# Another order of the first pieces of a linear-attention and mixture-of-experts kernel

## The chip, the cores and the metric

One core of a Trainium2 chip runs one program. The metric is the device time of the whole program in microseconds. The engines named below are TensorE (PE, its weight loads PEld), VectorE (DVE), ScalarE (ACT), GpSimd (POOL) and SyncE (SP), which here issues every DMA.

## The reference

A gated linear attention (4 batches, 8 heads, 768 tokens, head size 48) gives 3072 rows of 384 numbers. They go through a mixture of 8 experts whose mixing weights come from a gate, normalised by turns over rows and columns (8 times):

```python
for t in range(S):
    state = alpha[:, :, t, :, None] * state + np.einsum('bhd,bhe->bhde', k[:, :, t], v[:, :, t])
    y[:, :, t] = np.einsum('bhd,bhde->bhe', q[:, :, t], state)
x = y.transpose(0, 2, 1, 3).reshape(B * S, H * D)      # 3072 x 384
logits = x @ w_gate
P = np.exp(logits - logits.max())
for _ in range(8):
    P /= P.sum(1, keepdims=True) + 1e-09
    P /= P.sum(0, keepdims=True) + 1e-09
    P *= N / E
for e in range(8):
    out += P[:, e:e+1] * (np.maximum(x @ w1[e], 0.0) @ w2[e])   # w1 384x1024, w2 1024x384
```

## The kernel before, in words

**Attention.** The tokens are cut into units of 256 (3 for each of 4 batches) and these into chunks of 128 tokens, 24 in all. Chunks 0 to 3 (the first two units) are made by `direct_chunk`, step by step: the loads of alpha, k, q and v (`AN`, `KN`, `QN`, `VN`); the *turn*, in which TensorE transposes alpha, k and q into `psD`, `psTk`, `psQR`, ScalarE copies them out, and VectorE forms T = q times decay; six *levels* of 1 to 32 tokens, each with matmuls into `psl`, two products of T with the decay D, a predicated copy of the level's scores into A, and a *merge* that multiplies neighbouring decays (D2 from D1, and so on); level 64 with ScalarE's copies of A; the tail (`psy`, ScalarE's `ab` and `kb`); the normalisation and the carried state `ST`; the transposed x (`xT`); and the gate's matmul `psg`. The later chunks take their scores from *block units*: `attn_block` (b2, b3, ...) loads q, alpha and k of a unit as `qt`, `al`, `kt`, forms 16 products of neighbouring tokens (`tmp`, on GpSimd), which VectorE sums into `AB`, and multiplies decays into qt and kt.

**Experts.** The weights of the first three experts are loaded in the attention's time by `load_expert`: w1 and w2 through buffers named `xT`, squares on ScalarE, a scale s_w, and then four pieces of w1 and four of w2, each split into an upper half in float16 and the *lower half*, what the upper half lost. The lower half is made by VectorE (scalar_tensor_tensor), or by ScalarE and GpSimd. `work_gate` does the same with the gate's weights: a load `wgf`, its largest entry `wgm`, a scale, and the halves `wg`. `moe_tile` multiplies x by w1 and, after the ReLU, by w2, for 128 or 256 tokens at a time (`ps` matmuls); these tiles are what TensorE works on when nothing of the attention is ready.

**The order.** The program is written out by one string, `ORDER` (line 40). Its entries are called one after the other: `c0` the next step of chunk 0, `b2` of block unit 2, `w0` of expert 0's weights, `g` of the gate, `d3` the decays of unit 3, and `f` gives 0.45 us worth of tiles, if tiles are there. An entry in upper case sets `lop[0]`, which moves what may be done by either engine from VectorE to GpSimd: lower halves, merges of D, products of blocks. An entry that may not come yet (`early_`) is kept and tried again before each later one. Every engine runs its own instructions in the order in which they were written, and waits where an operand or a buffer isn't ready.

Of the kernel before, what the change touches and what calls it, by code (L numbers as in the profile page):

```python
# [25 lines left out]
def tile_gla_moe(ctx: ExitStack, tc: tile.TileContext, q, k, v, alpha, wg, w1, w2, out):  # L26
# [10 lines left out]
    NTT = NT // P  # L37
    NP = H // 2
    DP = 64
    ORDER = 'W1 C0 c1 C0 c0 f f f w1 f f f W0 f g f f f f f f f f w0 f f c0 f w0 c0 C1 C0 c1 C0 w0 c0 f f c1 f c2 C0 f f b2 b2 f f f f f f f w2 W0 f c1 w2 c1 f f f w0 b2 f f f C2 f f f f f f f f f f f f f f f f f f B2 f f f f f f f f f f w0 w0 w0 f f C3 f W2 c0 f f c1 c1 f f f f f f c1 C2 B2 b3 b2 f f C1 c2 d2 C0 C2 w2 f f f f f f C1 C0 C1 B2 f f f f c2 B2 f g f b2 f f w0 f f f f f f f f f f f f f f f f f f f f f f f f f f f f f f f f f f f f f f f f f f f f f f f f f f f f f f f f f f f f f f f f W0 f f f f f f f f f f f f f f f f f f f f f f f f f f f f f f f f f f f f f f f f f f f f f f f f f f f f f f f f f f f f f f f f f f f f c3 f f f f f f f f f f f f f f f f f f f f f f f f f f f f f f f f f f f f f f f f f f f f f f f f f f f f f f f f f f c2 f f f f f f C0 w2 w2 w2 W2 C3 f f f f f f f w0 f f f f f f f f f f f f f f f f f f f c2 f f f f f f f f f f f f f f f f f f f f f f f f f f f f f f f f f f f f f f f f f f f f f f f f f f f f f f f f f f f f f f f f f f f f C3 f f f f f f f f f f f f f f f f f f f f w1 f f f f f f f f f f f f f f f f f f f f f f f f f f f f f f f f f f C3 f f f f f f f f f f f f f f f f f f f f f f f f f f f f f f f f f f f f f f f f f f f f f f f f f f f f f f w0 f f f f f f f f f f f f f f f f f f f f f f f c2 f f f f f f f f f f f f f f f f f f f f f f f f f f f f f f f f f f f f f f f f f f f f W0 f B3 B3 C2 f f f C2 f f f f w0 b2 C2 f f f f f f g f f f C3 f W1 f f f f f f f f f f f f f f f f f f f f f f f f f f f f f b2 C1 f f f f f f f f f f f f f f f f f f f f b2 f f W0 f f f f f f f f f f f f f C3 f f f c3 f f b3 B2 f B2 W0 f f f B2 C4 C3 f f f f f f w1 f f g w2 D3 f f c3 c3 C3 w1 C2 f f f w1 f w1 f f f f f f f f f f f f f f B2 f W1 f f f b3 W1 f f f f f f f w1 f f f f f f f f c4 f f W1 f f w1 f f f B3 B3 W1 f f f f f f f f f f f f f f f f f f f f f f f f f f f f f f f f f f f f f f f f f f f f f f f f f f f f f f f f f f f f f f f f f f f f f f f f f f f f f f f f f f f f f f f f f f f f f f f f f f f f f f f f f f f f f w1 f f f f f f b4 f f f f f f f f c4 f f f f f f f f f f f f f f f f f f f f c4 f f f f f f f f f f f f f f f f f f f f f f f f f f f f f f f f f f f f f f f f f f f f f f f f f f f f f f f f f f f f f f f f f f f f f f f f w1 f f f f f c3 f f f f f f f f f f b3 f f c4 f f f f f f f f f f f f f f f f B3 f f f f f f f f B3 f c6 c5 B3 f f f b3 w2 f f f f f f b3 f f f f f b3 c4 f B3 f f w2 f c5 w2 f f f w2 f f f w2 c5 w1 C5 w2 f f f f f f f f f f f f f f f f f f c5 f f f f f f w2 f f f f f f B3 B4 f f f f f f f f f f f f f f f f f b4 f b4 f f f f f f f f f f f f f f b4 f f f f b4 b4 f f B4 f B4 c5 f f f f f f f f f f f b4 f B4 c6 f b4 f f f C8 f f f c6 f f B4 f f B4 C6 f f f f f c6 B4 f c7 B5 B4 f f f f c6 f c7 f f f f f f d4 f f f f f f f c7 f f c7 f f f f f f f f f b5 f C7 B5 b5 f f c8 f f f f C7 B5 f f f f f f f f f f b5 b5 f f f f f f f f f f f f f C9 f f c8 f f f f f f f B5 f f f f f f f b5 f f f f B5 B5 f f f t f b5 f f b5 f f f f f b5 f f b5 f f f f c8 c8 B5 c9 f f f f f f t c9 f f f B6 f f f f c9 f f f f f d5 f c8 f f f c9 f f f c10 f f f f f c9 f f f f c10 b6 f f f f f f f f b6 f f t f f f B6 f b6 f B6 f t f f f f f f f f B6 f f f f f f f c11 f f c10 f f f f f f f B6 f f f f f f f f f t f f b6 f f B6 f f f f b6 B6 f f f B6 b6 f b6 b6 B7 f f f f c10 f c11 f f f f f f f f t f f c11 f f f f c10 f f c11 f f f f f d6 f f f f c11 c12 f f f f f f f f c11 f f f f C12 c10 f f f b7 f f f f f f B7 f t f f B7 B7 f f f f f t f f B7 f f f f f f b7 f f f f f f f f c13 f f f c12 B7 f f f f f f f f f f B7 f f f f f f f f b7 f B7 f f f f B7 f f f B7 b7 f f b7 f f f c12 f c13 f f f f f f b7 f B8 c13 f f f f f f f c12 f f c13 f f f f d7 f f f f f c13 f f f f f c14 f f C13 f f f f C14 c12 f f f f f f f f b8 f f f f f f b8 f b8 B8 f f f f f B8 f f f f f f b8 f f c15 f f c14 f f f f f f B8 f f f f f f b8 f f f t f f f f B8 f f f f b8 f b8 f f B8 f B8 b8 f f f f f f B9 b8 f f c14 f c15 f f f f f f t c15 f f f f f f c14 f c15 f C15 f f f f f d8 f f f f B9 c16 f f f f f f f f c15 f f f f c16 c14 f f f f f b9 f f f f f f t f B9 f f B9 f f f B9 t f B9 f f f f f f f f f f f f f c17 f f c16 f f f f f f B9 f f f f f b9 f f f t f f f f B9 f f C17 f b9 B9 f f f b9 f f B9 b9 f f f b9 f f f f c16 f f f t f f f f B10 c17 f c16 f f f f f c17 f f f f f f d9 f f c17 f c18 f f f B10 f f f f f f c17 f f f f c16 c18 f f f f f f f b10 f f f f f t f f f B10 f f B10 f b10 t f f f f f f f b10 f f f f f f f f c19 f f f f f f f f f B10 f f f f f b10 f f f t f f f c18 f B10 B10 f f f f f b10 f B10 f f f B10 f f f f f f c18 b10 f c19 B10 f f f f t B11 c19 f f f f f f c18 f f c19 f f f f f f d10 f f f f c19 c20 f f f f f f f f c19 f f f f c20 c18 f f f f f f f f b11 f f f f f B11 f b11 f B11 f B11 b11 f f f f f f f f f f f f f f c21 f f c20 f f f f f f f B11 f f f f f b11 f f f t f f f f B11 f f f f b11 B11 f f b11 f f B11 b11 f f b11 f f f f f c20 f c21 f f f f f f t v c21 f f f f f f c20 f f c21 f f f f f d11 f f f f c21 c22 f f f f f f f f c21 f f f f c22 c20 f f f f f f f f f f f f f f f f f f f f f f f f f f f f f f c23 f f c22 f f f f f f f f f f f v f f f f t f v f f f f f f f f v f v f f f f f v f v f f f c22 f c23 f f f f f v f t v c23 f f f f f f c22 v f f c23 f f f f v f f f v f f c23 f f f f f v f f f c23 f f f f c22 f f f f f f f f f f f f f f f f'  # L40
    NA = 3

    pin = tc.keep_in_program_order
# [847 lines left out]
    w0, w1_, w2_ = (load_expert(e, wAB[e]) for e in range(NA))  # L891
# [85 lines left out]

    order = ORDER.split()
    while order:
# [582 lines left out]
```

## Time and profile before

| | us |
|---|---|
| median of three runs | 1655.36 |
| lowest and highest | 1650.81, 1655.67 |
| profiled execution | 1653.3 |
| its span in the trace | 1651.6 |
| TensorE busy in the span | 1596.8 (97%) |
| VectorE busy | 1271.7 (77%) |
| ScalarE busy | 930.8 (56%) |
| GpSimd busy | 375.1 (23%) |

The span is the time from the first to the last instruction that the profiler recorded; the execution's own time is 1.7 us longer. TensorE is busy in nearly all of it; the page's 40 slices show it less busy in the first three only (6, 6 and 8 tenths, at granted clocks of 6, 6 and 8 tenths), which is where attention and weights have to be made before tiles exist.

### The profile page before, as it was taken

How to read it: one execution, taken by the hardware profiler on the slowest of the kernel's cores; microseconds unless marked ns; L12 is line 12 of the kernel's file. 1: busy time of each engine (PE TensorE's matmuls, PEld its weight loads, DVE VectorE, ACT ScalarE, POOL GpSimd, SP SyncE). 2: the span in 40 equal slices, each digit the busy share in tenths (PEclk: the TensorE clock that was granted, in tenths of full speed). 3: DMA queues.
4: the chain of work that ended last, by engine and by line, in shares of the span. 5: the costliest groups of instructions: out<-in, count | busy, mean ns of one | idle time of the engine just before them, and what ended most of it. 6: DMA issues, size and time to landing. Idle time of an engine off the chain costs nothing.

```text
span 1651.6 us, 45345 instructions
## 1 busy us (share of the span) xinstructions
PE 1596.8 (97%) x18865; PEld 1376.3 (83%) x18865; DVE 1271.7 (77%) x2854; ACT 930.8 (56%) x2230; POOL 375.1 (23%) x382
## 2 busy tenths in 40 slices
PE   6689999999999999999999999999999999999999
PEld 5567777777777777777799999999999999999998
DVE  6868667665666666447778988998799879999997
ACT  4257543433443343434677777766776677665554
POOL 2325366557457656310000000000000000000000
PEclk6689999999999999999999999999999999999999
DMA  7244431542353343322253263235323543325443
GB/s 169 54 114 116 104 80 53 133 122 67 76 122 84 105 116 75 89 73 107 55 184 103 103 177 121 94 129 170 129 94 129 154 138 100 119 96 183 151 151 126
DMA packets 194655, 188.53 MB, mean 114 GB/s; under 512 B 115088, under 2 KB 175248, under 8 KB 194448
## 3 DMA queue, kind: packets, MB, share of 16 engines
q1 hardware_dynamic: 194448, 185.62, 38.1%
q8 instruction: 148, 2.42, 0.6%
q14 instruction: 59, 0.48, 0.1%
HBM read 129.76 MB, written 55.82 MB: 112 GB/s over the span
## 4 chain that ended last, share of the span: by engine, by line
PE 80%; DVE 10%; POOL 2%; ACT 2%; SPq 2%; issue 2%; DMA 1%; DVEq 0%; ACTq 0%; POOLq 0%
PE ps L66 28%; PE p1a L66 15%; PE p2x L66 12%; PE p2y L66 6%; PE p1c L66 4%; PE p1d L66 4%; PE p2v L66 3%; PE psy L66 2%; SPq L57 2%; PE psl L66 2%; DVE h L57 2%; POOL tmp L57 2%; DVE w L57 1%; DVE AB L57 1%; DVE hf L57 1%
## 5 line engine op out<-in xcount | busy, mean ns | idle before, releaser
L66 PEld LDWEIGHTS <-h 128*128 128x128 f16 x6768 | 593.1, 98 | 117.4 <-issue 6.7
L66 PEld LDWEIGHTS <-w 128*128 128x128 f16 x4896 | 464.2, 98 | 64.5 <-issue 13.4
L57 DVE TENSOR_TENSOR h<-hf,h 128x256 f16<-128x256 f32 x480 | 286.4, 616 | 31.8 <-ACT h L57 31.4
L66 PE MATMUL ps<-xT,w 128*128 128x256 f16 (+1 forms) x2664 | 300.0, 270 | 5.1 <-DVE h L57 3.6
L66 PE MATMUL ps<-w,h 128*128 128x384 f16 x1728 | 296.7, 327 | 2.3 <-POOL w L57 1.2
L66 PE MATMUL p1a<-x,w 128*128 128x256 f16 (+1 forms) x1860 | 289.3, 269 | 5.1 <-DVE p1d L57 3.0
L66 PE MATMUL p2x<-w,h 128*128 128x192 f16 x2832 | 272.0, 246 | 0.0
L57 ACT CAST h<-hf 128x256 f16<-128x256 f32 x480 | 250.7, 571 | 14.3 <-DVE hf L57 10.2
L57 DVE TENSOR_TENSOR hf<-hf 128x256 f32<-128x256 f32 x480 | 182.1, 420 | 29.7 <-ACT hf L57 24.9
L66 PE MATMUL p1a<-x,wx 128*128 128x256 f16 (+1 forms) x744 | 199.6, 269 | 0.0
L57 DVE SCALAR_TENSOR_TENSOR h<-ps,h 128x256 f16<-128x256 f32 (+1 forms) x296 | 114.5, 410 | 101.9 <-ACT h L57 100.9
L57 ACT ACTIVATE h<-ps 128x256 f16<-128x256 f32 (+1 forms) x296 | 110.4, 377 | 140.2 <-PE ps L66 139.4
L66 PEld LDWEIGHTS <-wx 128*128 128x128 f16 x1736 | 167.3, 98 | 17.3
L57 POOL TENSOR_TENSOR tmp<-qt,kt 128x768 f32<-128x768 f32 (+2 forms) x83 | 137.8, 1665 | 134.8 <-DMA kt<-in_k_dram 50.3
L57 ACT ACTIVATE hf<-p1d 128x256 f32<-128x256 f32 x120 | 46.0, 383 | 164.2 <-DVE h L57 140.5
L66 PE MATMUL p2y<-w,h 128*128 128x192 f16 x1416 | 136.1, 246 | 0.0
L57 DVE TENSOR_REDUCE AB<-tmp 128x16 f32<-128x768 f32 (+2 forms) x90 | 81.1, 903 | 68.6 <-POOL tmp L57 68.4
L57 ACT COPY r<-ps 128x384 f32<-128x384 f32 x72 | 34.3, 478 | 163.7 <-PE ps L66 129.5
L66 PE MATMUL p1c<-x,wx 128*128 128x256 f16 (+1 forms) x372 | 98.8, 269 | 0.0
L66 PE MATMUL p1d<-x,wx 128*128 128x256 f16 (+1 forms) x620 | 85.2, 269 | 0.0
L57 ACT ACTIVATE hf<-p1c 128x512 f32<-128x512 f32 x120 | 70.9, 591 | 0.0
L57 ACT COPY A<-psl 16x128 f32<-16x128 f32 (+3 forms) x148 | 49.2, 335 | 35.1 <-PE psl L66 30.7
(229 smaller groups left out, 1946.4 us busy)
## 6 DMA issues: line engine op xcount, KB each, us to landing
x<-xd SPq DMA_DIRECT2D x60, 704.0 KB, 5.4
accd<-acc SPq DMA_DIRECT2D x48, 384.0 KB, 3.2
acc<-accd SPq DMA_DIRECT2D x48, 384.0 KB, 3.2
raw<-r SPq DMA_DIRECT2D x72, 192.0 KB, 1.9
ri<-raw SPq DMA_DIRECT2D x72, 192.0 KB, 3.9
xT<-in_moe_w_dram SPq DMA_DIRECT2D x8, 768.0 KB, 5.0
w1f<-in_moe_w_dram SPq DMA_DIRECT2D x16, 384.0 KB, 7.5
w2f<-in_moe_w_dram SPq DMA_DIRECT2D x8, 768.0 KB, 6.9
```

The lines of the kernel that those rows point to most:

```text
L57: r = f(*a, **k_)
L66: tc.keep_in_program_order(nc.tensor.matmul(out_, lhsT, rhs, start=start, stop=stop, **k_))
```

## The change

Only the string changes. Its first entries (1150 before, 1900 now; the difference is 750 more `f`, which do nothing while no tile waits) are in another order; each chunk, block, expert and the gate has as many entries as before, and the last 1225 entries are the same. Some are in upper case that were not, and the other way round.

```diff
-    ORDER = 'W1 C0 c1 C0 c0 f f f w1 f f f W0 f g f f f f f f f f w0 f f c0 f w0 c0 C1 C0 c1 C0 w0 c0 f f c1 f c2 C0 f f b2 b2 f f f f f f f w2 W0 f c1 w2
...
+    ORDER = 'w2 W2 C0 f f C0 f f f f f w2 f f f D2 f f f f f f c4 f B2 f f f f f f f f f f f f f f f f f f f f f f f f w2 f f f f f f f f f f f f f f f f 
...
```

The order of SyncE's transfers at the start. AN, KN, QN, VN are a chunk's alpha, k, q, v; the buffers xT0_1, xT1_1 take an expert's w1, xT0_2, xT1_2 its w2; qt, al, kt are block unit 2's. Before:

```order
L57 DMA xT1_1_86<-in_moe_w1_dram 32x1024 x4
L57 DMA wgf_197<-in_moe_w_gate_dram 32x3x8 x4
L57 DMA xT0_2_84<-in_moe_w2_dram 128x4x384
L57 DMA xT1_2_87<-in_moe_w2_dram 128x4x384
L57 DMA AN_155<-in_alpha_dram 128x8x48
L57 DMA KN1_120<-in_k_dram 128x8x48
L57 DMA QN1_118<-in_q_dram 128x8x48
L57 DMA VN1_125<-in_v_dram 128x4x48 x2
L57 DMA qt_0_2_522<-in_q_dram 128x1x768
L57 DMA al_0_2_524<-in_alpha_dram 128x1x768
L57 DMA kt_0_2_523<-in_k_dram 128x1x768
```

After, from the same queue:

```order
L57 DMA VN0_124<-in_v_dram 128x4x48 x2
L57 DMA qt_0_2_230<-in_q_dram 128x1x768
L57 DMA al_0_2_232<-in_alpha_dram 128x1x768
L57 DMA kt_0_2_231<-in_k_dram 128x1x768
L57 DMA wgf_197<-in_moe_w_gate_dram 32x3x8 x4
L57 DMA AN_155<-in_alpha_dram 128x8x48
L57 DMA KN0_119<-in_k_dram 128x8x48
L57 DMA QN0_117<-in_q_dram 128x8x48
L57 DMA VN0_124<-in_v_dram 128x4x48 x2
```

Block 2's three loads moved from behind chunk 2's to directly behind chunk 0's; w1 moved behind the gate and chunk 1, w2 further back.

VectorE, at expert 0's second pair of w2 pieces (w21 is the lower half, T and A32 are levels of chunk 2 and 3, AB the sums of block 2). Before, from the last rows of chunk 3's level 4:

```order
L57 COPY_PREDICATED A32_0_3_1119<-odd_165,psl1_0_3_1102 128x64x2
L57 TENSOR_TENSOR T1_0_3_1061<-T1_0_3_1061,D4_0_3_1173 128x2x32x4
L57 SCALAR_TENSOR_TENSOR w21_0_297<-xT0_2_84,s_w2_0_1150,w20_0_296 128x768
L57 TENSOR_TENSOR T0_0_2_652<-T0_0_2_652,D64_0_2_1152 128x2x2x64
L57 COPY_PREDICATED A32_0_2_751<-odd_165,psl_0_2_734 128x8x32
L57 TENSOR_TENSOR T1_0_2_653<-T1_0_2_653,D64_0_2_1152 128x2x2x64
L57 TENSOR_TENSOR D128_0_2_1219<-D64_0_2_1152 128x4
L57 SCALAR_TENSOR_TENSOR w21_0_297<-xT1_2_87,s_w2_0_1150,w20_0_296 128x768
L57 TENSOR_REDUCE AB0_126<-tmp8_0_2_6_1022 128x4x8
L57 TENSOR_REDUCE oneg_wg_1283<-pst_wg_1280 1x1
L57 TENSOR_SCALAR oneg_wg_1283<-oneg_wg_1283 1x1
L57 TENSOR_SCALAR one_wg_1282<-oneg_wg_1283 1x1
```

After:

```order
L57 TENSOR_TENSOR T0_0_2_705<-T0_0_2_705,D64_0_2_1209 128x2x2x64
L57 COPY_PREDICATED A32_0_2_742<-odd_165,psl_0_2_725 128x8x32
L57 TENSOR_TENSOR T1_0_2_706<-T1_0_2_706,D64_0_2_1209 128x2x2x64
L57 TENSOR_TENSOR T0_0_3_965<-T0_0_3_965,D8_0_3_1164 128x2x16x8
L57 COPY_PREDICATED A32_0_3_1075<-odd_165,psl0_0_3_1057 128x32x4
L57 COPY_PREDICATED A32_0_3_1075<-odd_165,psl1_0_3_1058 128x32x4
L57 TENSOR_TENSOR T1_0_3_966<-T1_0_3_966,D8_0_3_1164 128x2x16x8
L57 TENSOR_REDUCE AB0_126<-tmp4_0_2_5_1187 128x4x4
L57 TENSOR_TENSOR qt_0_2_230<-qt_0_2_230,al_0_2_232 128x2x192
L57 TENSOR_TENSOR al_0_2_232<-al_0_2_232 128x2x48
L57 TENSOR_TENSOR tmp8_0_2_6_1283<-qt_0_2_230,kt_0_2_231 128x1536
L57 SCALAR_TENSOR_TENSOR w21_0_385<-xT0_2_84,s_w2_0_1238,w20_0_384 128x768
```

The gate's four steps on `oneg_wg` and `one_wg` are gone from here (they come in chunk 0's first levels now). Between chunk 2's last level (its products with D64) and the lower half of xT1_2 stood one merge, D128_0_2; now chunk 3's level 8, the sum of block 2's tmp4, its qt and al, and tmp8 stand there, ahead of both lower halves.

GpSimd, from the clearing of chunk 0's A on (D8_0_0 is chunk 0's D of 8 tokens, tmp block 2's products). Before:

```order
L57 MEMSET A_0_0_233 128x1024
L57 MEMSET A_0_1_370 128x1024
L57 TENSOR_TENSOR D16_0_0_372<-D8_0_0_324 128x32
L57 TENSOR_TENSOR D32_0_0_434<-D16_0_0_372 128x16
L57 TENSOR_TENSOR D128_0_0_505<-D64_0_0_457 128x4
L57 TENSOR_TENSOR tmp4_0_2_0_528<-qt_0_2_522,kt_0_2_523 128x768
L57 TENSOR_TENSOR tmp1_0_2_1_588<-qt_0_2_522,kt_0_2_523 128x384
L57 MEMSET A_0_2_670 128x1024
L57 TENSOR_TENSOR D2_0_2_753<-D1_0_2_650 128x256
```

After:

```order
L57 MEMSET A_0_0_228 128x1024
L57 TENSOR_TENSOR D8_0_0_334<-D4_0_0_281 128x64
L57 MEMSET A_0_1_380 128x1024
L57 TENSOR_TENSOR tmp4_0_2_0_382<-qt_0_2_230,kt_0_2_231 128x768
L57 TENSOR_TENSOR D2_0_1_433<-D1_0_1_360 128x256
L57 TENSOR_TENSOR D32_0_0_453<-D16_0_0_388 128x16
L57 TENSOR_TENSOR D4_0_1_476<-D2_0_1_433 128x128
L57 TENSOR_TENSOR D64_0_0_498<-D32_0_0_453 128x8
L57 TENSOR_TENSOR D8_0_1_519<-D4_0_1_476 128x64
L57 TENSOR_TENSOR D128_0_0_541<-D64_0_0_498 128x4
L57 TENSOR_TENSOR D16_0_1_558<-D8_0_1_519 128x32
```

The first product of block 2 (tmp4) moved ahead of nearly all merges, and the merges of chunk 0 and 1 that VectorE did (D8_0_0, D2_0_1, D4_0_1, D64_0_0 and others) are here now. In all, ten merges of D and three lower halves moved from VectorE to GpSimd: D of 128x256, 128x128, 128x16 and 128x4 one each, of 128x64 two, of 128x8 four.

## Rows read from the trace of the kernel before

**Rows 1.** Busy time by stretch: us and instructions, then clock, DMA share, GB/s.

```profile
core 0: us, PE busy (x) PEld busy (x) DVE busy (x) ACT busy (x) POOL busy (x), PEclk, DMA share, GB/s
0.00:10.00 10.00, 4.20 (x76) 3.26 (x76) 7.71 (x18) 3.29 (x6) 6.87 (x33) 1.00 0.84 169
0.00:118.83 118.83, 82.18 (x1532) 66.78 (x1533) 85.03 (x233) 47.45 (x102) 39.07 (x66) 0.71 0.44 109
118.83:192.68 73.85, 70.42 (x858) 53.99 (x857) 57.45 (x113) 48.16 (x111) 33.92 (x23) 1.00 0.41 107
192.68:1651.60 1458.92, 1444.25 (x16477) 1255.52 (x16476) 1129.17 (x2509) 835.21 (x2017) 302.13 (x293) 1.00 0.38 115
```

**Rows 2.** TensorE, 118 to 200 us: start, length, operation, [idle before, releaser].

```profile
118.83 7.91 PE L66 MATMUL ps<-xT,w 128*128 128x256 f16 x71 [0.55 <-DVE xT L57]
...
188.51 0.33 PE L66 MATMUL psy<-ab,onesb 128*128 128x128 bf16 x3 [1.15 <-ACT ab L57]
...
192.68 0.42 PE L69 MATMUL psd<-ident,DN 16*128 16x16 f32 x4
```

**Rows 3.** VectorE in time order, 0 to 119 us.

```profile
9.91 0.76 DVE L57 TENSOR_TENSOR T<-T,D 128x256 f32<-128x256 f32 x2 [0.56 <-PE psl L66]
10.59 0.42 DVE L57 TENSOR_TENSOR D<-D 128x256 f32<-128x256 f32 x1
...
17.92 0.76 DVE L57 TENSOR_TENSOR T<-psQR,D 128x256 f32<-128x256 f32 x2 [3.44 <-ACT QR L57]
...
36.73 0.95 DVE L57 TENSOR_REDUCE AB<-tmp 128x16 f32<-128x768 f32 x1 [4.77 <-POOL tmp L57]
...
88.64 2.57 DVE L57 SCALAR_TENSOR_TENSOR w<-xT,s_w,w 128x768 f16<-128x768 f32 x1 [5.36 <-ACT w L57]
```

**Rows 4.** Transfers issued by SyncE in time order, 0 to 60 us.

```profile
16.61 1.84 SPq L57 DMA_DIRECT2D wgf<-in_moe_w_gate_dram  x4
...
28.75 0.60 SPq L57 DMA_DIRECT2D kt<-in_k_dram  x1
```

**Rows 5.** GpSimd in time order, 0 to 119 us.

```profile
34.89 1.81 POOL L57 TENSOR_TENSOR tmp<-qt,kt 128x768 f32<-128x768 f32 x1 [9.51 <-DMA kt<-in_k_dram]
```

**Rows 6.** TensorE in time order, 0 to 119 us.

```profile
4.32 1.11 PE L69 MATMUL psD<-ident,AN 128*128 128x128 f32 x4 [4.32 <-POOL AN L57]
...
33.65 1.12 PE L69 MATMUL psD<-ident,AN 128*128 128x128 f32 x4 [0.68 <-ACT kb L57]
...
108.37 0.62 PE L66 MATMUL psg<-wg,xT 128*128 128x8 f16 x9 [1.57 <-ACT wg L57]
```

**Rows 7.** VectorE by shape, 0 to 119 us: busy, mean ns; idle before.

```profile
L57 DVE TENSOR_TENSOR T<-T,D 128x256 f32<-128x256 f32 x54 | 24.7, 460 | 6.7 <-PE psl L66 5.5 <-issue 1.1
L57 DVE SCALAR_TENSOR_TENSOR w<-xT,s_w,w 128x768 f16<-128x768 f32 x7 | 9.2, 1340 | 5.4 <-ACT w L57 5.4
L57 DVE COPY_PREDICATED A<-odd,psl 128x128 f32<-128x128 int32 x24 | 6.8, 347 | 0.0
...
L57 DVE TENSOR_TENSOR qt<-qt,al 128x384 f32<-128x384 f32 x4 | 2.2, 558 | 0.0
```

**Rows 8.** ScalarE in time order, 0 to 119 us.

```profile
7.26 0.59 ACT L57 COPY QR<-psQR 128x512 f32<-128x512 f32 x1 [0.24 <-PE psQR L69]
```

**Rows 9.** GpSimd by shape, 0 to 119 us: busy, mean ns; idle before.

```profile
L57 POOL TENSOR_TENSOR tmp<-qt,kt 128x768 f32<-128x768 f32 x5 | 9.2, 1833 | 19.5 <-DMA kt<-in_k_dram 9.5 <-DVE qt L57 5.1 <-DVE AB L57 4.9
...
L57 POOL TENSOR_TENSOR w<-xT,w 128x768 f16<-128x768 f32 x2 | 4.0, 1994 | 13.5 <-ACT w L57 13.5
...
L57 POOL TENSOR_TENSOR D<-D 128x256 f32<-128x256 f32 x2 | 3.4, 1676 | 0.0
L57 POOL TENSOR_TENSOR D<-D 128x64 f32<-128x64 f32 x2 | 0.8, 404 | 1.5 <-DVE D L57 1.4
```

**Rows 10.** VectorE in time order, 118 to 200 us.

```profile
135.24 1.79 DVE L57 TENSOR_TENSOR qt<-qt,al 128x384 f32<-128x384 f32 x1
```

**Rows 11.** GpSimd in time order, 118 to 200 us.

```profile
134.54 2.07 POOL L57 TENSOR_TENSOR A<-an,mask 128x1024 f32<-128x1024 f32 x1
```

2 lines of the change are left out of this document (1 added, 1 removed).

## The prediction

> **What bounds the kernel now.** I read the table by stretch first. From 192.68 us on TensorE is busy 1444.25 of 1458.92 us at a granted clock of 1.00; before 118.83 it is busy 82.18 of 118.83 at 0.71; between the two, 70.42 of 73.85 [rows 1]. The two marks come from TensorE's own rows: 118.83 is where the first tile of full length begins, 192.68 the first decay matmul of block unit 3 [rows 2]. From that matmul on, both orders put the same instructions in the same places on every engine, so the change is worth exactly the difference in the time at which this point is reached, and the 1458.92 us behind it stay.
>
> Ahead of 118.83 no engine is full: VectorE is busy 85.03 us [rows 1], the most of all. So VectorE's waits are what can be won, and its rows in time order come next. The long ones are 3.44 us at 17.92 (chunk 1's QR from ScalarE), 4.77 at 36.73 (the first product of block unit 2, from GpSimd) and 5.36 at 88.64 (a scaled piece of expert 0's w2, from ScalarE); short ones of about 0.56 (hand-offs from TensorE's level results) come again and again [rows 3]. The one at 36.73 goes back further: GpSimd's product waited 9.51 us for kt [rows 5], and SyncE issued kt's load only at 28.75, behind the weights and the gate [rows 4].
>
> **What the change removes.** It deletes and adds no work; it moves steps and gives some from VectorE to GpSimd.
> - Block 2's loads now stand straight behind chunk 0's on SyncE, some 20 us earlier, so kt is there when GpSimd comes to the product. VectorE's 4.77 goes: −4.8.
> - Expert 0's w2. The lower halves on VectorE still wait for ScalarE, but now eight other VectorE rows stand between: one level of chunk 3 (two rows of 0.46, two of 0.347: 1.6), one reduction of a product (0.95 as at 36.73), qt (0.558), al (half of that, 0.26) and tmp8, a product twice as long as the 0.95 of a row with 768 elements (1.75). Together 5.1 of the 5.36 [rows 3, 7]; I take −5.4 at first, since the wait's source, ScalarE's queue, starts earlier too, and leave the difference of 0.3 to the range.
> - The gate's preparation (the letter g) is done some 80 us earlier. TensorE's wait of 1.57 at 108.37 for wg goes [rows 6]: −1.6.
> - The gate's small VectorE rows (a reduction and four one-element steps) fall into the wait of 3.44 at 17.92 [rows 3]; they stood in full work before: −1.0, an estimate of five rows of some 0.2 each.
>
> Sum: −12.8.
>
> **What it adds.**
> - VectorE's row wgm (largest gate weight) now stands in chunk 0's second level and must wait for wgf. Ahead of it on SyncE stand chunk 0 (four tensors of 128x384 floats, 0.79 MB) and block 2 (three of 128x768, 1.18 MB). At the 169 GB/s of the first 10 us [rows 1] they land at 11.6; a last small load 0.8 later gives 12.4. VectorE comes to wgm when its D of 128x256 ends, 10.59 + 0.42 = 11.0 [rows 3]. Wait: +1.3; below, 0, if the loads overlap better than in those 10 us; above, 2.5, if chunk 1's loads share the bandwidth. Behind wgm on VectorE stand all of chunk 0's next levels.
> - Chunk 2's turn (12 transposes, four copies, the products with D) now stands behind chunk 0's normalisation instead of beside VectorE's wait for block 2 (it began at 33.65 [rows 6], VectorE waited until 36.73). Chunk 0's turn shows its length with buffers free: 4.32 to 7.26 + 0.59, 3.5 [rows 6, 8]. Chunk 1 gives VectorE one level meanwhile: 0.460 × 2 + 0.347 × 2 = 1.6 [rows 7]. With 0.5 for the step from the normalisation to the first transpose, 3.5 + 0.5 − 1.6 = +2.4 (0 if other rows cover it all, 4.2 if none does and the copies queue).
> - Merges of D on GpSimd. Ten more than before: one of 128x256 at 1.68, nine at no more than the 0.40 of a 128x64, at 0.3 each 2.7; together 4.4 [rows 9]. VectorE is spared 0.42 [rows 3] and nine of some 0.2: 2.1. A merge is needed only by the next level but one, so most of it lies beside VectorE's rows. Three more lower halves on GpSimd take 3 × 1.99 = 6.0 there [rows 9] and 3 × 1.34 = 4.0 less on VectorE [rows 7]. They are needed by tiles that come after 118.83, and GpSimd, busy 39.07 of 118.83 [rows 1], has the room; if that cover is gone, a tile waits for one half, 2.0. Against it: while GpSimd reads its operands, VectorE can stand still. qt of 128x384, 0.558 on average [rows 7], took 1.79 at 135.24 [rows 10], with GpSimd's A (134.54 to 136.61) beside it [rows 11]. What VectorE is spared and what it is stopped for are of one size; net +1.0, bounds −2.1 (all spared, none stopped) and +4.0.
> - The stretch from 118.83 to 192.68 is TensorE's, with 3.43 us without work [rows 1], 1.15 of it at 188.51 for ab [rows 2]. Here the new order puts ScalarE's ab of chunk 4 behind three w2 pieces and expert 1's scale behind four squares. TensorE's queue of tiles covers most of it: +1.0 (0 to 4, four waits of the size at 188.51).
> - Hand-offs. Two chunks are interleaved in another way, and I count two or three more of the 0.56 [rows 3]: +1.3.
>
> Sum: +7.0. The whole: −12.8 + 7.0 = −5.8. The profiled execution took 1653.3 (span 1651.6 and 1.7 around it), so 1647.5; the median of the runs stands 2.1 above that one: 1649.6.
>
> **Weighing a rule.** The case's row is the qt above: 1.79 instead of 0.558 beside GpSimd's A [rows 7, 10, 11]. The Trainium skill, page "SBUF — State Buffer", section "SBUF: two separate sides", says that VectorE and GpSimd share a port pair as an exclusive lock, and that a VectorE instruction with two SBUF inputs is fully held up by a GpSimd instruction that reads SBUF, for the whole of it. The row agrees in that qt ended after A did; by the rule each added GpSimd row stops VectorE wholly, and the term of +1.0 would be that of the first rival below.
>
> **Rivals.**
> 1. *GpSimd's added rows stop VectorE (slower).* Place: levels of chunks 0 to 3. Price: GpSimd's added 4.4 + 6.0, and its tmp of 1.83 [rows 9], beside which VectorE had nothing to do before, stop VectorE for 12.2 us; spared are 2.1 + 4.0, net +6.1. The level behind a late merge waits for the difference of the two engines' merges, 4.4 − 2.1 = +2.3. The rows that should fill the wait of 5.36 are stopped too, so that gain isn't had. −4.8 − 1.6 − 1.0 + 6.1 + 2.3 + the other additions (1.3 + 2.4 + 1.0 + 1.3 = 6.0) = +7.0: 1662.4. It decides from the point where more than half of the 12.2 falls on VectorE rows with two inputs in SBUF. For it: qt's row; T and D rows, 24.7 us of T alone [rows 7], have such inputs. Against it: VectorE's rows that read PSUM or one input lie between, and it had 33.8 us idle.
> 2. *No change.* The waits for block 2 and for ScalarE are paid by what VectorE meets behind them: the same chain of levels of chunks 0 to 3 must end before the tiles start. If 4.77 and 5.36 come back by half in hand-offs and in the turn of chunk 2, the sum is −5.8 + 5.1 = −0.7: 1654.7. For it: the hand-offs, 5.5 us altogether [rows 7], are waits of a dependence chain, not of a full engine.
> 3. *Larger gain.* Turn and hand-offs are hidden by the other chunk's rows, GpSimd's help is worth 0.5 instead of costing 1.0: −12.8 + 1.3 (wgm) + 1.0 (118 to 192) − 0.5 = −11.0, so 1644.4. For it: VectorE's 33.8 idle us of 118.83 leave room.
>
> That the order doesn't do what it says is excluded by the listing of both: on SyncE, VectorE and GpSimd the instructions stand as told.
>
> **Chances.** My forecast (−2 to −10) 0.50, no change 0.24, slower 0.14, larger gain 0.12. The likeliest case's own range is 1645 to 1654. The bounds of the additions (0 − 2.1 + 0 + 0 against 2.5 + 4.2 + 4.0 + 4.0 + 1.3) span −14.9 to +3.2; with rival 1 the range reaches to 1659, and below to 1642. This kernel's measurement tells a difference from none at about 0.3%, 5 us. My forecast lies on that edge: 0.32 of its 0.50 are beyond 5 us, with the 0.12 that gives faster 0.44; slower is rival 1, at +7.0 mostly beyond it, and the tail of rival 2: 0.17; the rest, 0.39, is the same.
>
> **What would show it.** In the changed kernel's rows, 192.68 becomes about 186.9 and the 1458.9 behind stay. VectorE's waits at block 2's first reduction and at w2's first lower half are under 1 us; psg waits for nothing; wgm waits about 1.3; the first tile of full length starts at about 112. Rival 1 shows as means: T over 0.460, qt over 0.558, GpSimd's D over 1.68 in the first 119 us. I am wrong if block unit 3's first decay starts later than 192.68, or if TensorE's waits between the marks pass 7 us.

## The result and the profile after

The changed kernel takes 1637.2 us (median; 1636.43 to 1639.26); before took 1654.26. The ratio is 0.9902, interval [0.9883, 0.9921]: 16 us faster (13 to 19). The forecast was 5.8 less, so 1649.6 with a range of 1645 to 1654; 1637.2 lies under it. The profiled execution took 1637.29, its span is 1635.6 (before 1651.6).

The table by stretch of the changed kernel, cut at the same two events as before [rows 1, 2]: the first tile of full length (now at 100.64) and block unit 3's first decay (now at 178.92).

```profile
0.00:100.64 100.64, 75.39 (x1532) 61.27 (x1533) 83.61 (x224) 46.74 (x101) 41.37 (x76) 0.85 0.49 124
100.64:178.92 78.28, 75.25 (x858) 55.89 (x857) 57.26 (x111) 51.34 (x115) 40.28 (x26) 0.93 0.49 120
178.92:1635.60 1456.68, 1442.30 (x16477) 1254.79 (x16476) 1126.44 (x2509) 835.20 (x2017) 301.52 (x293) 1.00 0.38 114
```

Against before, the first stretch became 18.19 us shorter, the second 4.43 longer, the rest 2.24 shorter. TensorE executes the same 1532 and 858 matmuls in the first two. VectorE is busy 83.61 us in the first stretch against 85.03: what went is its idle time, 33.8 to 17.0. The first 8 us blur this sum a little: there one copy's row is long in some profiles (3.75 us for three copies before) and a wait of about 4 us stands in its place in others, while the product behind starts at 7.88 to 8.07 in all of them. Counted from 7.85 us on, idle went from 32.1 to 14.5. TensorE's granted clock, as a share of full speed, rose in the first stretch (0.71 to 0.85) and fell in the second (1.00 to 0.93).

VectorE in time order, the rows that answer to [rows 3]:

```profile
12.81 0.18 DVE L57 TENSOR_REDUCE wgm<-wgf 128x1 f32<-128x24 f32 x1 [1.06 <-DMA wgf<-in_moe_w_gate_dram]
...
16.09 1.65 DVE L57 TENSOR_TENSOR T<-T,D 128x256 f32<-128x256 f32 x1
18.66 0.76 DVE L57 TENSOR_TENSOR T<-psQR,D 128x256 f32<-128x256 f32 x2 [0.91 <-ACT QR L57]
...
28.72 0.94 DVE L57 TENSOR_REDUCE AB<-tmp 128x16 f32<-128x768 f32 x1
...
36.91 0.76 DVE L57 TENSOR_TENSOR T<-psQR,D 128x256 f32<-128x256 f32 x2 [0.51 <-ACT QR L57]
...
74.89 2.30 DVE L57 SCALAR_TENSOR_TENSOR w<-xT,s_w,w 128x768 f16<-128x768 f32 x1
```

Block 2's first sum (28.72) and w2's lower half (74.89) wait for nothing; they waited 4.77 and 5.36. The gate's wgm waits 1.06 for its load. Chunk 1's QR is waited for 0.91 instead of 3.44, but the product with it starts at 18.66, 0.74 later than before (17.92): VectorE comes to it later. Chunk 2's (36.91) is waited for 0.51; before, that product started at 42.00 without a wait, because VectorE was kept by other rows until then.

TensorE, the rows that answer to [rows 2, 6]:

```profile
34.27 0.66 PE L69 MATMUL psD<-ident,AN 128*128 128x128 f32 x4
...
35.60 0.66 PE L69 MATMUL psQR<-ident,QN 128*128 128x128 f32 x4 [0.24 <-ACT D L57]
...
64.72 0.17 PE L66 MATMUL psg<-wg,xT 128*128 128x8 f16 x1 [2.16 <-ACT wg L57]
66.23 0.35 PE L66 MATMUL psg<-wg,xT 128*128 128x8 f16 x8 [1.34 <-DVE wg L57]
...
100.64 0.58 PE L66 MATMUL ps<-xT,w 128*128 128x256 f16 x2 [0.55 <-DVE xT L57]
```

In the kernel before, chunk 2's turn went one group of transposes at a time, each waiting for ScalarE's copy of the last:

```profile
35.44 1.12 PE L69 MATMUL psTk<-ident,KN 128*128 128x128 f32 x4 [0.68 <-ACT D L57]
37.29 1.12 PE L69 MATMUL psQR<-ident,QN 128*128 128x128 f32 x4 [0.74 <-ACT T L57]
```

Now it goes through with one wait of 0.24, from 34.27 to 36.3. The wait for wg before the first psg is not gone but earlier and longer (2.16, then 1.34). SyncE and ScalarE in the first 30 us, to [rows 4, 8]:

```profile
5.55 0.60 SPq L57 DMA_DIRECT2D kt<-in_k_dram  x1
6.19 2.01 SPq L57 DMA_DIRECT2D wgf<-in_moe_w_gate_dram  x4
...
13.03 10.37 SPq L57 DMA_DIRECT2D xT<-in_moe_w_dram  x18
```

```profile
16.19 0.59 ACT L57 COPY D<-psD 128x512 f32<-128x512 f32 x1 [8.34 <-PE psD L69]
...
18.04 0.59 ACT L57 COPY QR<-psQR 128x512 f32<-128x512 f32 x1 [0.35 <-PE psQR L69]
18.93 0.84 ACT L57 ACTIVATE w<-xT 128x768 f16<-128x768 f32 x1 [0.31 <-DMA xT<-in_moe_w_dram]
```

SyncE issues w1 from 13.03, five us later than before, and ScalarE makes chunk 1's copies (16.19 to 18.6) ahead of w1's squares (18.93). Before, the first two squares stood ahead of those copies:

```profile
12.99 0.84 ACT L57 ACTIVATE w<-xT 128x768 f16<-128x768 f32 x1 [5.15 <-DMA xT<-in_moe_w_dram]
...
15.47 0.57 ACT L57 COPY D<-psD 128x512 f32<-128x512 f32 x1
```

Last, by shape, VectorE and GpSimd, to [rows 7, 9]:

```profile
L57 DVE TENSOR_TENSOR T<-T,D 128x256 f32<-128x256 f32 x54 | 24.5, 470 | 2.6 <-PE psl L66 2.6
...
L57 DVE TENSOR_TENSOR qt<-qt,al 128x384 f32<-128x384 f32 x4 | 2.2, 549 | 0.0
```

```profile
L57 POOL TENSOR_TENSOR w<-xT,w 128x768 f16<-128x768 f32 x2 | 4.7, 2362 | 6.4 <-ACT w L57 6.4
...
L57 POOL TENSOR_TENSOR D<-D 128x256 f32<-128x256 f32 x3 | 2.2, 733 | 0.0
```

The mean of T went from 460 to 470 ns, that of qt from 558 to 549: on average VectorE was not stopped more than before. Single rows are stretched: the T at 16.09 took 1.65 us instead of some 0.45 and ended 0.3 us after a GpSimd product that ran beside it:

```profile
15.65 1.82 POOL L57 TENSOR_TENSOR tmp<-qt,kt 128x768 f32<-128x768 f32 x1
```

### The profile page after: what moved, and what is told of

The parts are those of the page before. It is cut to its first block, busy times and chain, and to the rows that moved or that the text cites. A ratio compares the mean times of both kernels' runs of the same rounds, so it can differ in the third digit from the quotient of the medians.

```text
span 1635.6 us, 45368 instructions
## 1 busy us (share of the span) xinstructions
PE 1592.9 (97%) x18865; PEld 1372.0 (84%) x18865; DVE 1267.3 (77%) x2841; ACT 933.3 (57%) x2233; POOL 383.2 (23%) x395
## 4 chain that ended last, share of the span: by engine, by line
PE 82%; DVE 10%; POOL 3%; issue 2%; ACT 2%; DMA 1%; SPq 0%; DVEq 0%; POOLq 0%; ACTq 0%
PE ps L66 29%; PE p1a L66 15%; PE p2x L66 12%; PE p2y L66 6%; PE p1c L66 4%; PE p1d L66 4%; PE p2v L66 3%; PE psl L66 2%; PE psy L66 2%; POOL tmp L57 2%; DVE h L57 2%; DVE w L57 1%; DVE hf L57 1%; DVE acc L57 1%; DVE AB L57 1%
## 5 line engine op out<-in xcount | busy, mean ns | idle before, releaser
L57 POOL TENSOR_TENSOR tmp<-qt,kt 128x768 f32<-128x768 f32 (+2 forms) x83 | 138.6, 1674 | 125.6 <-DMA kt<-in_k_dram 40.3
L57 ACT COPY r<-ps 128x384 f32<-128x384 f32 x72 | 34.4, 479 | 163.0 <-PE ps L66 129.6
```

The source lines that it names most:

```text
L57: r = f(*a, **k_)
```

## The experiments

Each is given against before by the ratio of their runs, in us at 1654. "Mark" is the start of the first long tile in its one profile, "idle" VectorE's idle time from 7.85 us up to there, "decay" the start of block unit 3's first decay. The diffs show the steps in the order in which they are executed, without `f`; w0.3 is expert 0's third step.

| run | ratio, interval | us | mark | idle | decay |
|---|---|---|---|---|---|
| before | 1 | 0 | 118.83 | 32.1 | 192.68 |
| before_block2_loads_early | 1.0004 [0.9995, 1.0013] | +0.7 | 121.57 | 34.8 | 197.27 |
| before_squares_behind_turn | 0.9994 [0.9982, 1.0007] | −1.0 | 121.31 | 35.0 | 196.81 |
| before_loads_and_squares | 0.9972 [0.9959, 0.9985] | −4.6 | 116.20 | 29.4 | 191.92 |
| before_loads_squares_w2 | 0.9986 [0.9973, 1.0] | −2.3 | 118.14 | 30.2 | 193.41 |
| before_loads_squares_w2_gate | 1.0014 [1.0004, 1.0024] | +2.3 | 119.89 | 32.5 | 195.65 |
| before_four_steps | 0.9995 [0.9985, 1.0005] | −0.8 | 119.77 | 32.1 | 193.63 |
| before_norm_ahead | 0.9973 [0.9959, 0.9987] | −4.5 | 113.15 | 25.9 | 186.98 |
| before_norm_and_chunk3 | 0.9984 [0.9972, 0.9996] | −2.6 | 115.98 | 28.7 | 189.84 |
| before_new_engines | 1.0028 [1.0017, 1.004] | +4.6 | 121.47 | 34.4 | 201.90 |
| changed kernel | 0.9902 [0.9883, 0.9921] | −16.2 | 100.64 | 14.5 | 178.92 |
| after_old_engines | 0.99 [0.9887, 0.9914] | −16.5 | 102.96 | 14.2 | 179.51 |
| after_block2_loads_late | 0.9986 [0.9977, 0.9995] | −2.3 | 114.77 | 29.7 | 191.57 |
| after_squares_ahead | 0.9934 [0.9909, 0.9958] | −10.9 | 106.50 | 20.3 | 183.34 |
| after_w2_early | 0.9952 [0.9934, 0.997] | −7.9 | 110.25 | 23.3 | 188.25 |
| after_chunk0_levels_first | 0.9926 [0.9907, 0.9944] | −12.2 | 105.29 | 17.9 | 180.35 |
| after_norm_behind | 0.9928 [0.9905, 0.9952] | −11.9 | 104.82 | 18.2 | 181.58 |
| after_clock_filler | 0.9885 [0.987, 0.9901] | −19.0 | 100.67 | 14.6 | 176.14 |

From 7.85 us on VectorE is busy 77.2 to 80.9 us up to the mark in all of them, so the mark moves with its idle time. Mark and decay come from one execution each, the ratio from all.

**Block 2's loads.** Theory A: removed waits are paid back by what VectorE meets next. Theory B: TensorE's clock decides. In the kernel before, SyncE's order alone:

```diff
-C0.1 c1.1 C0.2 ... C0.9 b2.1 b2.2
+C0.1 b2.1 c1.1 C0.2 ... C0.9 b2.2
```

> The kernel before, in which only block unit 2's three loads are issued earlier on SyncE (directly behind chunk 0's loads); no other engine's order changes. The prediction's first step alone: VectorE's wait of 4.77 us for block 2's first product goes, so 4.8 us less (about 1649.5). Theory A, waits are paid back by what VectorE meets next: 0 to 2 us less. Theory B, TensorE's clock decides: the time goes only as far as the stretch at half clock (11 to 55 us) becomes shorter; if it stays, 0 to 2 us less, if it ends earlier, more than 4.8.

It was worth nothing (+0.7). ScalarE's first square of w1 and VectorE's first product of chunk 1, in that run:

```profile
18.28 0.84 ACT L57 ACTIVATE w<-xT 128x768 f16<-128x768 f32 x1 [10.44 <-DMA xT<-in_moe_w_dram]
```

```profile
22.68 0.76 DVE L57 TENSOR_TENSOR T<-psQR,D 128x256 f32<-128x256 f32 x2 [7.47 <-ACT QR L57]
```

The 1.18 MB push w1 back; ScalarE stands at w1's first square for 10.44 us (5.15 before), with chunk 1's copies queued behind, and VectorE waits 7.47 for QR instead of 3.44. Chunk 2's QR is waited for 1.85 where before there was no wait. The gain of 4.77 was exchanged. Theory B fell as well: by the granted clocks of the two profiles TensorE ran at half clock for some 68 of the first 193 us before and for 27 of 197 here, and the time is the same. The executions of the kernel before say so without any edit: 96 of them, in five series, had mean granted clocks of 0.973 to 0.993, and the 38 at 0.981 or less took only 0.9 us longer on average, against their series' means, than the 42 at 0.986 or more.

The same step undone in the changed kernel, with block 2's first product (b2.2) behind the loads:

```diff
-C0.1 C0.2 B2.1 ... C1.2 b2.2 ... c2.1 c3.1 b2.3
+C0.1 C0.2 ... C1.2 ... c2.1 c3.1 B2.1 b2.2 b2.3
```

> The changed kernel, in which block 2's loads and first product come only behind chunk 2's loads again. The first step undone: 4.8 us more (about 1642). If the step is worth nothing in the new order: within 1 us of the changed kernel. Theory B: more than 4.8 if TensorE's half-clock stretches (41 us in 0 to 179) grow.

13.9 us were lost, not 4.8. GpSimd and VectorE there:

```profile
39.38 1.80 POOL L57 TENSOR_TENSOR tmp<-qt,kt 128x768 f32<-128x768 f32 x1 [18.52 <-DMA kt<-in_k_dram]
```

```profile
41.22 0.95 DVE L57 TENSOR_REDUCE AB<-tmp 128x16 f32<-128x768 f32 x1 [13.07 <-POOL tmp L57]
```

In the new order that sum stands earlier on VectorE (28.7, not 36.7), so the late load is waited for 13.07 us.

**The squares on ScalarE.** Theory D: these squares hold chunk 1's copies until w1 lands. Theory E: the gain is one of hand-offs all over.

```diff
-w0.2 c0.4 w0.3 c0.5 C1.2 C0.6
+w0.2 c0.4 c0.5 C1.2 w0.3 C0.6
```

> The kernel before, in which only ScalarE's order changes: the first two squares of expert 0's w1 come behind chunk 1's four copies, as in the changed kernel. Theory D (ScalarE waits at these squares for w1's transfer, and chunk 1's turn behind them): VectorE's wait of 3.44 us for chunk 1's QR falls to about 1, 2 to 3 us less at that place, paid back at least in part by the wait for block 2's first product, whose loads are still late: 0 to 3 us less in all. Theory E (the gain is of hand-offs between the chunks all over): within 1 us of before.

> The kernel before with both: block 2's loads directly behind chunk 0's on SyncE, and the squares of w1 behind chunk 1's copies on ScalarE. Theory D: the earlier loads alone gave nothing because they delay w1, for which ScalarE holds chunk 1's copies (VectorE's wait for QR 3.44 became 7.47); with the squares out of the way both waits go, 4.77 + 3.44 less a rest of 1: 6 to 8 us less than before. Theory E: within 2 us of before.

Alone it gave −1.0, within noise; with the loads −4.6, less than the 6 to 8 of theory D but not nothing: neither edit alone can be told from nothing. The other way round, in the changed kernel (w0.2 and w0.3 ahead of C1.2):

> The changed kernel, in which only ScalarE's order changes: the first two squares of expert 0's w1 stand ahead of chunk 1's four copies, as before. In the changed kernel SyncE issues w1 from 13.03 us on, 5 later than before. Theory D: ScalarE holds chunk 1's copies until w1 lands (about 18 instead of 13), VectorE's wait for QR grows from 0.9 to 5 or more: 4 to 8 us more than the changed kernel. Theory E: within 1 us of it.

5.3 us lost (−16.2 to −10.9; the two intervals just overlap). ScalarE and VectorE there:

```profile
19.88 0.84 ACT L57 ACTIVATE w<-xT 128x768 f16<-128x768 f32 x1 [11.84 <-DMA xT<-in_moe_w_dram]
```

```profile
24.06 0.76 DVE L57 TENSOR_TENSOR T<-psQR,D 128x256 f32<-128x256 f32 x2 [5.49 <-ACT QR L57]
```

ScalarE waits 11.84 for w1, VectorE 5.49 for QR, and the product with it starts at 24.06 instead of 18.66: theory D as told.

**w2's lower half, and the gate.**

```diff
-C2.10 w0.15 b2.10 g.3 C3.6 b2.11 b2.12 W0.16
+C2.10 b2.10 g.3 C3.6 b2.11 b2.12 w0.15 W0.16
```

> As the kernel with both, and the lower half of w2's third piece stands behind chunk 3's level 8 and two sums of block 2 on VectorE (the wait of 5.36 us at 88.64 gets other work ahead of it). The prediction's second step: 5.4 us less than the kernel with both, some 11 to 13 less than before. If VectorE waits for something else there: 0 to 2 us less.

2.3 us more than without it, which the intervals don't tell from nothing; the 5.4 of the prediction are not there. VectorE:

```profile
86.94 0.28 DVE L57 TENSOR_REDUCE oneg_wg<-pst_wg 1x1 f32<-1x128 f32 x1 [3.84 <-PE pst_wg L69]
...
95.63 0.29 DVE L57 SCALAR_TENSOR_TENSOR h<-ps,h 128x128 f16<-128x128 f32 x1 [2.72 <-ACT h L57]
```

The wait of 5.9 for w became 3.84 for the gate's transposed maximum, which stands behind chunk 2's tail on TensorE, and 2.72 for h, whose tile stands on TensorE behind matmuls that wait 1.48 for that half of w2. With the gate's steps early, too (g.1 and g.2 behind c0.3, g.3 behind c0.4, g.4 behind b2.10):

> As the kernel before with early block-2 loads, late squares and the late lower half of w2 (which was 1.9 us under before, 2.2 over the one without the last edit), and the gate's four steps early, as in the changed kernel. There VectorE's wait of 5.9 for w2's piece had become one of 3.84 for the gate's pst_wg and one of 2.72 for ScalarE's h. If the gate's row was in the way: the 3.84 goes and the time falls by 3 to 5 us, to some 6 to 9 under before. Theory F: 0 to 1 us less, the wait moves on to the next row that needs chunk 2's tail or the tile.

4.6 worse again: there wgf was issued behind chunk 1's loads, and VectorE stood at wgm for longer than any bound of the prediction:

```profile
17.17 0.18 DVE L57 TENSOR_REDUCE wgm<-wgf 128x1 f32<-128x24 f32 x1 [5.97 <-DMA wgf<-in_moe_w_gate_dram]
```

The same with wgf directly behind block 2's loads, and g.4 where it was:

> The kernel before with all four of the prediction's removals where they can take effect: block 2's loads directly behind chunk 0's, the gate's load directly behind these (not behind chunk 1's, where VectorE waited 6.0 us for it), the squares behind chunk 1's copies, the late lower half of w2, and the gate's rows in chunk 0's first levels. The prediction's removals would make 12.8 us less, less 1.3 for the gate's load. Theory J: the chunks' own chain takes it back, 2 to 6 us under before.

−0.8: early loads, late squares, w2's half and the gate's rows, all in the old order of the chunks, are together worth nothing. (Of the prediction's removals one is missing here: the wait of 1.57 for wg before the first psg stays, because g.4 does.) VectorE there, behind chunk 2's last level:

```profile
87.45 0.43 DVE L57 TENSOR_TENSOR T<-T,D 128x256 f32<-128x256 f32 x1 [3.34 <-issue]
...
96.39 0.29 DVE L57 SCALAR_TENSOR_TENSOR h<-ps,h 128x128 f16<-128x128 f32 x1 [3.73 <-ACT h L57]
```

The wait moves on again, to 3.34 and 3.73. In the changed kernel, with w2's pieces straight behind chunk 2's last level:

```diff
-C2.9 C3.6 b2.9 W0.13 w0.14 B2.10 b2.11
+C2.9 W0.13 w0.14 C3.6 b2.9 B2.10 b2.11
```

> The changed kernel, in which w2's first two pieces of expert 0 come straight behind chunk 2's last level again, ahead of chunk 3's level 8 and of block 2's rows (VectorE's and GpSimd's order change, TensorE's and ScalarE's don't). The prediction's second step undone: VectorE waits some 5 us for ScalarE's piece again, 5.4 us more than the changed kernel (about 1642.5). Theory F, such a wait is only exchanged for the next one of the same chain: 0 to 2 us more.

8.3 us lost, most of it in two waits:

```profile
76.85 1.66 DVE L57 SCALAR_TENSOR_TENSOR w<-xT,s_w,w 128x768 f16<-128x768 f32 x1 [4.37 <-ACT w L57]
...
92.69 0.29 DVE L57 SCALAR_TENSOR_TENSOR h<-ps,h 128x128 f16<-128x128 f32 x1 [2.90 <-ACT h L57]
```

**Engines.** The k-th step of each piece has the other kernel's case, nothing else moves.

> The order of before with the changed kernel's choice of engine: each piece has the upper or lower case that it has in the changed kernel (ten more merges of D and three more lower halves on GpSimd); TensorE's order is that of before. The prediction: 1 us more (bounds 2.1 less to 4.0 more). Theory C, the excess of the gain comes from VectorE's relief: 6 to 11 us less. The port rival: 7 us more.

> The changed kernel's order with before's choice of engine; TensorE's and SyncE's order is that of the changed kernel. The prediction: 1 us less (4.0 less to 2.1 more). Theory C: 6 to 11 us more. If the order alone makes the gain: within 2 us of the changed kernel, some 16 us under before.

+4.6 in the old order, 0.3 less in the new one with the old choice: the other choice of engine is no source of the gain, and the order alone makes it. Theory C (VectorE's relief) fell, and so did the port rival's 7 us in the new order. The 4.6 of the old order have a reason in the rows of GpSimd and VectorE:

```profile
34.42 1.80 POOL L57 TENSOR_TENSOR tmp<-qt,kt 128x768 f32<-128x768 f32 x1 [13.69 <-DMA kt<-in_k_dram]
36.18 0.85 POOL L57 TENSOR_TENSOR D<-D 128x64 f32<-128x64 f32 x2
```

```profile
36.51 0.42 DVE L57 TENSOR_TENSOR T<-T,D 128x256 f32<-128x256 f32 x1 [7.78 <-POOL D L57]
```

A merge that VectorE needs now stands on GpSimd behind a product that waits 13.69 for block 2's late load, and VectorE waits 7.78 for it. In the changed kernel, where that load is early, VectorE waits for no such merge.

**The chunks' own order.** Theory G: alternating chunks hide hand-offs. In the changed kernel C0.7, C0.8 and C0.9 go behind c0.6, ahead of C1.3:

> The changed kernel, in which chunk 0's levels 8 to 32 stand together ahead of chunk 1's levels and no longer alternate with them (VectorE's and TensorE's order change there alone). Theory G, rows of the other chunk hide the hand-offs between VectorE and TensorE: some 6 to 8 hand-offs of 0.56 come back in chunks 0 and 1, 3 to 5 us more than the changed kernel. If the hand-offs don't matter: within 1 us.

4.0 us lost, as expected, but the intervals of the two overlap; VectorE's idle time went from 14.5 to 17.9. Theory K: chunk 0's normalisation ahead of chunk 2's turn is a gain, not a cost. The turn's transposes have two buffers in turn (`psa`, line 269 of the kernel), and chunk 0's unfinished psy holds one of them. In the old order (with loads and squares) and taken back in the new one:

```diff
-c0.10 C2.2 c1.7 c1.8 c1.9 C2.3 B2.5 b2.6 c2.4 C0.11 C1.10
+c0.10 C0.11 C2.2 c1.7 c1.8 c1.9 C2.3 B2.5 b2.6 c2.4 C1.10
```

> The kernel before with early block-2 loads and late squares (4.1 us under before), in which chunk 0's normalisation (psy, m, st, ys, pw, pss, ST) moves ahead of chunk 2's turn, as in the changed kernel. The prediction's added term: 2.4 us more than without this edit. Theory K: psy and pss leave the two buffers that the turn's transposes need, so the turn no longer goes one transpose at a time (5.4 us becomes under 3) and chunk 1's tail, which needs chunk 0's state, starts earlier: 2 to 5 us less than without it, 6 to 9 under before.

> The changed kernel with chunk 0's normalisation behind chunk 2's turn and first two levels again. The prediction's added term undone: 2.4 us less than the changed kernel. Theory K: 3 to 8 us more.

In the old order the profile's mark came 3.0 earlier than without it (116.20 to 113.15), but the time did not move beyond the noise (−4.6, −4.5). This run does not test the theory, though: TensorE and VectorE there,

```profile
36.93 0.66 PE L69 MATMUL psTk<-ident,KN 128*128 128x128 f32 x4 [0.68 <-ACT D L57]
38.32 1.12 PE L69 MATMUL psQR<-ident,QN 128*128 128x128 f32 x4 [0.74 <-ACT T L57]
```

```profile
37.77 0.28 DVE L57 TENSOR_SCALAR m<-psy 128x128 f32<-128x128 f32 x1
```

VectorE comes to the normalisation only at 37.77, behind three lower halves, so psy keeps its buffer and the turn still goes one group at a time. In the new one 4.3 were lost, with VectorE's wait for chunk 2's QR at 2.51 instead of 0.51 (intervals overlapping again):

```profile
38.06 0.75 DVE L57 TENSOR_TENSOR T<-psQR,D 128x256 f32<-128x256 f32 x2 [2.51 <-ACT QR L57]
```

With chunk 3's turn (c3.2) behind B2.7 and its first level (C3.3) behind c2.6, too:

> As the one with chunk 0's normalisation ahead, and chunk 3's turn and first level stand some 15 to 20 us earlier, directly behind chunk 1's tail and chunk 2's level 4, ahead of w2's squares and of chunk 2's later levels, as in the changed kernel (there chunk 3's first products stand at 53.6, before at 72.0). Theory K, going on: chunk 3's chain, which ends the stretch before the first long tile, starts earlier and is covered by chunk 2's levels: 3 to 8 us less than without it. If VectorE's other waits take it back: 0 to 2 us less.

1.9 more than without it, within noise: an earlier chunk 3 is no gain by itself.

**Weights against chunks.** Two exchanges were to tell whether the weights' places (theory I) or the chunks' order (theory J) makes the gain.

> The chunks' and blocks' order of before, with block 2's loads early, and the weights' and the gate's steps where the changed kernel has them among the chunk and block steps (counted by these steps). Theory I, the place of the weights' pieces and of the loads makes the gain: 10 to 16 us under before. Theory J, the way in which the chunks' steps stand among each other makes most of it: 3 to 6 us under before, as with the early loads and late squares alone.

> The chunks' and blocks' order of the changed kernel with its gate steps and the first four steps of expert 0 (loads, squares), and all other weight steps where before has them among the chunk and block steps. Theory I: 6 us or more above the changed kernel. Theory J: within 4 us of the changed kernel.

Both came out slower than before (1.0643 [1.0627, 1.0659] and 1.006 [1.0045, 1.0075]) and tell nothing of the two theories: in the first TensorE is busy only 72 and 70 of the 100 us from 100 and from 200 on, against 92 and 98 before. Whether either part needs the other is not shown by mixtures that are slower for reasons of their own.

**The clock.** Theory H: the half clock costs the second stretch. In `attn_tail`, ahead of the gate's matmuls:

```diff
         psg = psa.tile([P, 512], F32, tag="psa", name=f"psg_{nm}")
+        for _ in range(14 * (b == 0 and ch in (2, 3, 4))):
+            mm(psg[:, :P], onesb, onesb)
```

> The changed kernel with 14 extra matmuls of 128 columns (about 0.06 us each, 0.8 us per place) ahead of the gate's matmuls of chunks 2, 3 and 4, where TensorE otherwise waits for VectorE and its granted clock then fell to half (at 100 and 138 us). They write into psg, which is overwritten. Theory H, the half clock costs the stretch that is TensorE's (10.2 us of it, so 5 us): 2 to 5 us less than the changed kernel if the clock stays, up to 2 us more if it falls all the same.

2.8 us less than the changed kernel (1634.23, all runs 1632.14 to 1636.05, against 1636.43 to 1639.26): the lowest ratio of all, though the two intervals overlap. TensorE around the place, in the changed kernel and with the filler:

```profile
135.95 0.97 PE L66 MATMUL ps<-w,h 128*128 128x384 f16 x5 [1.18 <-DVE w L57]
137.78 0.37 PE L66 MATMUL psg<-wg,xT 128*128 128x8 f16 x9 [0.86 <-DVE ys L57]
...
139.07 7.96 PE L66 MATMUL ps<-w,h 128*128 128x384 f16 x30
```

```profile
134.52 0.97 PE L66 MATMUL ps<-w,h 128*128 128x384 f16 x5 [1.18 <-DVE w L57]
136.36 0.94 PE L66 MATMUL psg<-onesb 128*128 128x128 bf16 x14 [0.87 <-DVE ys L57]
...
137.79 5.04 PE L66 MATMUL ps<-w,h 128*128 128x384 f16 x30
```

and the filler's second stretch, to be held against 78.28 at 0.93:

```profile
100.67:176.14 75.47, 72.16 (x888) 55.70 (x887) 57.16 (x112) 50.98 (x115) 40.29 (x26) 1.00 0.50 120
```

The 14 matmuls fill 0.94 us; 30 matmuls behind them take 5.04 instead of 7.96. The whole stretch is 2.8 us shorter, with 30 more matmul records in it.

## Why the prediction was wrong

*What bounds it* held: the change is decided ahead of block 3's first decay, by VectorE's idle time. Behind it 2.2 us went that the prediction put at nothing; the instructions are the same, and the stretch had between 1454.8 and 1459.2 in the profiles of the table.

For the first stretch the terms make −6.8 (mark at 112); it became 18.2 shorter. VectorE's idle time from 7.85 us up to the mark, by what it waited for:

| waited for | before | changed |
|---|---|---|
| block 2's products (tmp) | 7.1 | 0 |
| w2's piece | 5.4 | 0 |
| level results (psl) | 5.5 | 3.1 |
| QR of chunks 1 to 3 | 3.4 | 1.7 |
| psy (normalisation) | 3.7 | 2.2 |
| wg | 1.2 | 0.4 |
| nothing that the profile shows (issue) | 1.1 | 0 |
| h | 2.4 | 3.0 |
| w1m's or w2m's maximum (pst_w) | 0.3 | 1.1 |
| wgf | 0 | 1.1 |

*Removed.* Block 2's wait (−4.8) and w2's (−5.4) are gone, as forecast. The gate's −1.6 was a wait of TensorE, priced as if it were VectorE's: on TensorE it moved to 64.72 and 66.23, and VectorE's own wait for wg fell by 0.8. The gate's rows do stand ahead of chunk 1's QR now, as the prediction says (−1.0): VectorE comes to it 3.3 later, by these rows, by the wait for wgf (1.06) and by the stretched T at 16.09. That, and not an earlier QR, is why the wait there is 2.5 shorter.

*Added: the steps that failed.* The prediction booked "Hand-offs ... two or three more ... +1.3" and "Chunk 2's turn ... +2.4". The hand-offs in front of T, ten of 5.5 us, became five of 2.6: the term has the wrong sign. Undoing the alternation of chunks 0 and 1 cost 4.0. The turn had taken 5.4 us with one of its two buffers held by psy; behind the normalisation it takes 2.6, and VectorE waits 0.51 for it, not 2.4. (Of the 2.8 saved some 1.4 goes with TensorE's granted clock, 0.50 before and 1.00 now: the three groups took 1.12 each before and 0.60 to 0.66 now.) Taking that back cost 4.3. The intervals of both these runs overlap the changed kernel's, so their prices are rough. The sum also left standing what went too: two other waits of 2.3 for block 2's products and 1.5 of the wait for psy.

The gate's load is nearly right (1.06 for 1.3); no run shows by themselves the 0.8 us for the last small load and the 0.5 from the normalisation to the turn. The engines' +1.0 is within its bounds (the 2.1 us that GpSimd's merges were to spare add up to 2.2). The +1.0 of the second stretch was 4.4. Where the clock stayed at 1.00 in the new order (after_chunk0_levels_first) that stretch took 75.06, only 1.2 over 73.85, with TensorE's waits 1.0 longer, as forecast; the other 3.2 go with the fall of the clock, which the prediction doesn't mention.

*Missing.* The squares of w1 moved behind chunk 1's copies on ScalarE. The prediction shows SyncE, VectorE and GpSimd at this place, not ScalarE, and has no term for it. The move doesn't bring chunk 1's QR ahead of its time in the kernel before; it keeps the later w1 from holding it back. Without it 5.3 are lost.

*The sum itself.* Each removal was priced at its wait and the prices were added. In the new order these removals came nearly whole. But they belong to that order: put alone into the old one they gave +0.7, −1.0, −4.6 for two, −0.8 for four; taken alone out of the new one, the edits cost 13.9, 5.3, 8.3, 4.0 and 4.3, together 36 for a gain of 16. A wait on VectorE lies in front of the next one: removing it alone moves the wait on (7.47 for QR, 3.84 for the gate, 3.34 and 3.73), and putting one back into an order without others can cost more than the wait was worth before.

Rival 3, the larger gain (1644.4, chance 0.12), had the right reason ("hidden by the other chunk's rows") and still came out 7 us too slow. Rival 1's stop is there in single rows (1.65 for a T at 16.09), but the means that were to show it are 470 for 460 ns, 549 for 558 and 733 for 1676: the 12.2 us that it foresaw are not there.

Open: the best part of the new order that was rebuilt in the old one gave 4.6 of 16.2. The rest was not found in one piece, the normalisation's place was never tested there with the buffer free, and the two exchanges did not divide it.

## What to carry to other kernels

Where an in-order engine is idle more than a quarter of the time in many waits (here 33.8 of 118.83 us), read the order of every engine that feeds it at the moved place, the one off the path first (here ScalarE): a load moved ahead delays another load, and whoever waits for that one holds all that is queued behind. Don't add up waits as if each were free to go; price the order's whole idle time between "each is only exchanged" and "busy time alone". Work that is moved to another engine inherits what that engine waits for (here a merge behind a product whose load is late). Two chains that alternate seem to hide each other's hand-offs, and a chain that holds a buffer that the next one needs seems better finished than kept open; for both the rows are clear and the times only just.

## What the runs showed of the hardware

TensorE's granted clock fell to its lower level behind gaps of about 1 us in otherwise full work: in the changed kernel behind waits of 1.18 and 0.86 at 134.8 to 137.8 (0.50 from 138.6 to 145). But not always: with the old choice of engine similar gaps (1.52 and 0.70) left it at full speed, and the 30 matmuls behind took

```profile
141.03 5.04 PE L66 MATMUL ps<-w,h 128*128 128x384 f16 x30
```

Where TensorE is full, the lower clock shows in the time: in the old order, with the old engines, the second stretch took 73.8 to 73.9 at a granted clock of 1.00 and 75.3 to 75.8 at 0.98. Where VectorE's chain decides, it cost next to nothing (0.9 us between the executions of before at low and at high mean clock).

A VectorE product with both inputs in SBUF can be stretched beside a GpSimd product: 1.65 us for some 0.45 at 16.09. GpSimd's profiled time for one shape is no constant: D of 128x256 took 1676 ns on average before and 733 now, the lower half 1994 and 2362. What decides it, no run here shows.
